# Another written order of steps, and PSUM as one tile whose banks the list schedule hands out

## The chip, the cores and the metric

The kernel runs on one core of a Trainium2 chip. A core has a tensor engine (PE), a vector engine (DVE), a scalar engine (ACT), GpSimd (POOL) and a sync engine (SP), each with its own queue of instructions that it works off in order, and 16 DMA engines. PE writes its products to PSUM, a small memory of eight banks of 128 x 512 fp32 values; DVE and ACT read them from there. Engines wait for each other through semaphores. The metric is the device time of one execution in microseconds; less is better.

## The reference

An attention with exponential features, then a mixture of eight experts whose routing weights are normalized by eight rounds over rows and columns.

```python
def phi(x):                                   # x: 8 x 8 x 576 x 64
    proj = np.einsum('bhsd,df->bhsf', x, w_phi)
    proj = proj - np.max(np.abs(proj), axis=-1, keepdims=True)
    return np.concatenate([np.exp(proj), np.exp(-proj)], axis=-1)
q_p, k_p = (phi(q), phi(k))
kv = np.einsum('bhsf,bhsd->bhfd', k_p, v)
z = np.sum(k_p, axis=2)
num = np.einsum('bhsf,bhfd->bhsd', q_p, kv)
den = np.einsum('bhsf,bhf->bhs', q_p, z)[..., None] + 1e-06
x = (num / den)                               # as 4608 x 512
P = np.exp(x @ w_gate - logits_max)           # 4608 x 8
for _ in range(8):
    P /= P.sum(1, keepdims=True) + 1e-09
    P /= P.sum(0, keepdims=True) + 1e-09
    P *= N / E
for e in range(8):
    out += P[:, e:e + 1] * (np.maximum(x @ w1[e], 0.0) @ w2[e])
```

## The kernel before

The Python program does not issue instructions as it goes. Each piece of work is recorded as an `Op` of a `Plan`, with its engine, a guessed duration, what it reads and writes, and the buffers that it takes. `Plan.schedule` then walks through a list schedule: again and again it takes, of all operations whose inputs are there, the one that can start first by the guessed durations, and among equals the one recorded first. The instructions are issued in that order, so it fixes the order of every engine's queue. The guessed durations serve that order alone; on the chip an instruction starts when its semaphores say so.

Buffers come from rings: a `Ring` has a name, a shape and a number of slots, and a `Buf` is one use of a slot. A `Buf` gets its slot when its first operation is scheduled and gives it back after its last. In before the PSUM is a ring "P1" of eight slots, one bank each, with a tile of its own for each use; a second ring "P2" of double width has none. `Plan.start` asks whether slots are free and from when; `schedule` takes the slot with the earliest time of becoming free. An operation that touches a bank which another engine touched last starts after that one.

The attention works on 32 pairs of heads, four in each of the eight batches, in these steps, one letter each:

- "a" (`pair_a`, `scores`): the products of the keys with w_phi (line 407, `P<-wphi,qkT`), the maxima of their absolute values on DVE (line 399), four exponentials on ACT (line 403), and v scaled by the exponentials of the maxima on POOL (lines 532 and 537). It also issues the loads for the next batch.
- "q" (`queries`): the same for the queries, once with rows and once with features on the partitions.
- "r" (`rest_a`): keys and queries of the last 64 rows of a batch.
- "b" (`pair_b`): the product of k's features with v (line 407, `P<-v,k`), its copy out of PSUM, kv (line 587), and the numerators and denominators of the queries (lines 606 to 631). Line 587 is the "kv copy", one to a pair, 32 in all.
- "c" (`pair_c`): the transposes into xT (lines 645 and 648).
- "g" (`rest_c`, `gate`): the transposes of the last rows and the routing logits of a batch.

Two more letters are the first expert on batches that are done: "u" (`up0`) is eight matmuls of 512 columns into two banks with the ReLU on ACT (line 699), "d" (`down0`) eight matmuls into one bank, copied out by ACT (line 734) or DVE (line 741). The string `order` (line 814) says in which order these steps are recorded, and so which of two ready operations goes first. After it the routing runs on DVE, while PE works off what is left of the first expert. Then come the other seven experts, by products of 256 columns with sums and differences (line 1019, lines 927 to 1181), in a fixed order of its own. The weights of the experts, v, and intermediate results travel by DMA from the queues of POOL and SP.

Of the kernel before, what the change touches and what calls it, by code (L numbers as in the profile page):

```python
# [9 lines left out]
FP32 = mybir.dt.float32  # L10
# [7 lines left out]
class Buf:  # L18


    def __init__(self, ring):
        self.ring, self.t, self.slot, self.left, self.end = ring, None, None, 0, 0.0
        self.last = None

    def __call__(self):
        if self.t is None:
            self.t = self.ring.make(self.slot)
        return self.t


class Ring:


    def __init__(self, pool, shape, dtype, tag, bufs, psum=False):
        self.psum = psum
        self.free = [(0.0, i) for i in range(bufs)]
        self.make = lambda i: pool().tile(shape, dtype, name=tag, tag=f"{tag}_{i}")

    def new(self):
        return Buf(self)  # L40


class Op:
    __slots__ = ("eng", "dur", "lat", "nbytes", "fn", "left", "ready", "users", "idx", "end",
                 "bufs", "deps", "shared")

    def after(self, user):

# [5 lines left out]
class Plan:  # L54
# [43 lines left out]
    def start(self, o, free):  # L98

        t = max(free, o.ready, self.port if o.shared else 0.0)  # L100
        need = {}
        for b in o.bufs:
            if b.slot is None:
                n = need[b.ring] = need.get(b.ring, 0) + 1
                if len(b.ring.free) < n:
                    return None
                t = max(t, sorted(b.ring.free)[n - 1][0])
            elif b.last is not None and b.last.eng != o.eng:
                t = max(t, b.last.end)
        return t  # L110

    def schedule(self):
        ready = {}
        free = {}
        dma_free = 0.0
        for o in self.ops:
            if o.left == 0:
                ready.setdefault(o.eng, []).append(o)
        done = []
        while len(done) < len(self.ops):  # L120
            best = None
            for eng, rq in ready.items():
                f = free.get(eng, 0.0)
                if best is not None and f > best[0]:
                    continue
                for o in rq:
                    t = self.start(o, f)
                    if t is not None and (best is None or (t, o.idx) < best[:2]):
                        best = (t, o.idx, o)
            assert best is not None, "no operation can start"  # L130
            at, _, o = best
            ready[o.eng].remove(o)
            for b in o.bufs:
                if b.slot is None:
                    s = min(b.ring.free)
                    b.ring.free.remove(s)
                    b.slot = s[1]
            free[o.eng] = at + o.dur
            if o.shared:
                self.port = at + o.dur  # L140
            if o.nbytes:
                dma_free = max(at + o.dur + 1.0, dma_free) + o.nbytes / 1e3
                o.end = dma_free + 1.0
            else:
                o.end = at + o.dur + o.lat
            for b in o.bufs:
                if b.ring.psum:
                    b.last = o
                b.left -= 1
                b.end = max(b.end, o.end)  # L150
                if b.left == 0:
                    b.ring.free.append((b.end, b.slot))
            done.append(o)
            for u in o.users:
                u.left -= 1
                u.ready = max(u.ready, o.after(u))
                if u.left == 0:
                    ready.setdefault(u.eng, []).append(u)
        return done
# [9 lines left out]
def kernel(  # L169
# [33 lines left out]
    ps = ctx.enter_context(tc.tile_pool(name="ps", bufs=1, space=PSUM))  # L203
# [6 lines left out]
    P = const.tile([128, NT, E], FP32, name="P")  # L210
# [30 lines left out]
    def pool(el, fn, r=(), w=()):  # L241
        plan.op("POOL", el * 1.64e-3 + 0.17, 0.25, fn, r, w, shared=True)
# [5 lines left out]
    R = {}  # L248

    def ring(p, shape, dtype, tag, bufs):  # L250
        R[tag] = Ring((lambda: p) if not isinstance(p, str) else (lambda: late[p]),
                      shape, dtype, tag, bufs, p is ps)
# [31 lines left out]
    ring("s_p", [128, NT], FP32, "rr", 1)  # L284
    ring("s_p", [128, E], FP32, "cs", 1)
    ring("s_p", [128, E], FP32, "c_bc", 1)
    ring(ps, [128, 1024], FP32, "P2", 0)
    ring(ps, [128, 512], FP32, "P1", 8)

    def new(tag):  # L290
        return R[tag].new()

    def bf(buf):

# [111 lines left out]
    def mm(out_, lhsT, rhs, start, stop):  # L406
        nc.tensor.matmul(out_, lhsT=lhsT, rhs=rhs, start=start, stop=stop)  # L407
# [339 lines left out]
    for b in range(2):  # L747
# [58 lines left out]
    def stage_g(b):  # L806
# [5 lines left out]
             "c": lambda j: pair_c(j // 4, j % 4, xbs[j]), "g": stage_g,  # L812
             "u": lambda i: up0(i // 4, i % 4), "d": lambda i: down0(i // 4, i % 4)}
    order = (
        "aqraqabbcqabqacbqrbcaqbacuqaqbacqruabgqccucbudbduaqabdqadgrcbucqucabqcauqdua"
        "bgcbqaducdcqubcrbaudqauqdacbcdqduardqbbgcubuaqcaubgcdqacdqabubruqadbqadcbqbu"
        "cagcquaubqrdbadqaudbcqcaucbdcccqbgcg"
    )
    for i, n in enumerate(order):
        STEPS[n](order[:i].count(n))  # L820
# [22 lines left out]
    o = plan.op("X", 0.0, 0.0, swap, w=["late"])  # L843
# [270 lines left out]
    def down7(e, g, hT, B7):  # L1114
# [38 lines left out]
        def read(bank, i, j):  # L1153

            if e == 0:
                return start(bank, i, j)
            for n in range(2):
                ts = 2 * i + n
                dve(330, lambda n=n, ts=ts: nc.vector.scalar_tensor_tensor(  # L1159
                    out=acc[g][:, ts, 256 * j:256 * j + 256],  # L1160
                    in0=bank()[:, 256 * n:256 * n + 256], scalar=P[:, 4 * g + ts, e:e + 1],
                    in1=acc[g][:, ts, 256 * j:256 * j + 256], op0=ALU.mult, op1=ALU.add),
                    [bank, "P"], [("acc", g, ts, j)])
# [113 lines left out]
```

## Time and profile before

| | us |
|---|---|
| median of three runs (lowest, highest) | 1043.96 (1043.56, 1044.01) |
| span of the profiled execution | 1043.5 |
| PE busy | 1020.4 (98%) |
| DVE busy | 823.9 (79%) |
| ACT busy | 711.1 (68%) |
| POOL busy | 461.5 (44%) |
| idle time of PE | 23.1 |

The span is the time from the first to the last instruction of the profiled execution, which is another one than the three that were timed. A row of the timeline gives the start of a group of equal instructions, their time, engine, line, operation, what is written and read, the shape and the number. A row of the groups gives busy time, the mean of one, and the idle time of the engine ahead of them with what ended it. The granted clock of PE was 1.00 throughout.

### The profile page before, as it was taken

To read this page: it belongs to the slowest core of one execution; us is meant where nothing else is said; L and a number is where in the kernel's file an instruction comes from. 1 tells how busy PE (TensorE), PEld (TensorE's weight loads), DVE (VectorE), ACT (ScalarE), POOL (GpSimd) and SP (SyncE) were. 2 spreads that over 40 slices of the span, in tenths; PEclk is the share of its full clock that TensorE was granted. 3 is DMA by queue.
4 is the path that set the end of the run, shared out by engine and by line. 5 is a ranking of instruction groups with operands and counts; after the bars stand their busy time and mean duration, and the time that the engine had idled before them with its cause. 6 is when DMAs were issued, how large, how long until landed. Compare 5 with 4: busy or idle time off the path is not lost.

```text
span 1043.5 us, 24529 instructions
## 1 busy us (share of the span) xinstructions
PE 1020.4 (98%) x9512; PEld 842.1 (81%) x9512; DVE 823.9 (79%) x1626; ACT 711.1 (68%) x1570; POOL 461.5 (44%) x532
## 2 busy tenths in 40 slices
PE   6899999999999999999999999999999999999998
PEld 4566666654788888888888888888888888888886
DVE  6999899998777787778877787778777877787775
ACT  7999999944976666666666666565666666666663
POOL 3876757500233344344444444444444443333442
PEclk9999999999999999999999999999999999999999
DMA  9997987734411152113311441134111611114333
GB/s 250 150 196 132 150 127 136 122 122 120 93 41 41 52 105 60 51 42 82 81 41 42 87 87 51 42 69 95 41 42 50 125 51 42 41 43 131 122 122 122
DMA packets 105237, 93.94 MB, mean 90 GB/s; under 512 B 45344, under 2 KB 80288, under 8 KB 105120
## 3 DMA queue, kind: packets, MB, share of 16 engines
q1 hardware_dynamic: 71840, 68.45, 23.6%
q0 software_dynamic: 33120, 23.86, 16.4%
q8 instruction: 74, 1.21, 0.5%
q14 instruction: 43, 0.35, 0.1%
q10 hardware_dynamic: 160, 0.07, 0.0%
HBM read 94.98 MB, written 14.16 MB: 105 GB/s over the span
## 4 chain that ended last, share of the span: by engine, by line
PE 89%; ACT 5%; DVE 3%; DMA 1%; issue 1%; SPq 0%; POOL 0%; DVEq 0%; ACTq 0%
PE P L1019 70%; PE P L407 16%; ACT acc L1181 2%; DVE m L399 1%; PE P L606 1%; ACT k L403 1%; DMA acc<-in_q_dram 1%; DMA wgate_f<-in_moe_w_gate_dram 1%; ACT V L1171 1%; ACT U L1047 1%; PE P L645 1%; DVE xb L626 0%; ACT q L403 0%; DVE P L618 0%; PE P L484 0%
## 5 line engine op out<-in xcount | busy, mean ns | idle before, releaser
L1174 POOL TENSOR_TENSOR acc<-acc,V 128x512 f32<-128x512 f32 x248 | 316.4, 1283 | 440.4 <-ACT V L1171 437.2
L1051 DVE CUSTOM_DVE_ANT_0 hT<-P,U 128x512 bf16<-128x512 f32 x378 | 255.0, 687 | 107.9 <-ACT U L1047 59.7
L1047 ACT COPY U<-P 128x512 f32<-128x512 f32 x378 | 217.8, 590 | 137.4 <-PE P L1019 130.8
L1171 ACT ACTIVATE V<-P,P 128x256 f32<-128x256 f32 x496 | 206.3, 477 | 123.4 <-PE P L1019 121.6
L1159 DVE SCALAR_TENSOR_TENSOR acc<-P,P,acc 128x256 f32<-128x256 f32 x372 | 160.1, 478 | 73.4 <-PE P L1019 71.7
L1019 PEld LDWEIGHTS <-w 128*128 128x128 bf16 x2016 | 197.3, 98 | 23.7 <-issue 0.6
L1019 PEld LDWEIGHTS <-S 128*128 128x128 bf16 x1984 | 194.1, 98 | 23.2 <-issue 0.6
L1019 PEld LDWEIGHTS <-T 128*128 128x128 bf16 x1512 | 147.9, 98 | 19.1 <-issue 2.0
L1019 PEld LDWEIGHTS <-hT 128*128 128x128 bf16 x1488 | 145.4, 98 | 18.3 <-DVE hT L1051 1.1
L1019 PE MATMUL P<-X,w 128*128 128x256 bf16 x1008 | 154.7, 273 | 0.4 <-ACT U L1047 0.4
L1019 PE MATMUL P<-xT,w 128*128 128x256 bf16 x1008 | 152.0, 273 | 0.0
L1019 PE MATMUL P<-X,T 128*128 128x256 bf16 x1008 | 148.6, 273 | 1.3 <-ACT U L1047 1.2
L1019 PE MATMUL P<-w,hT 128*128 128x256 bf16 x992 | 142.6, 273 | 0.6 <-DVE hT L1051 0.6
L1019 PE MATMUL P<-T,S 128*128 128x256 bf16 x1056 | 136.3, 273 | 0.4 <-ACT V L1171 0.4
L1019 PE MATMUL P<-w,S 128*128 128x256 bf16 x928 | 126.6, 273 | 0.0
L532 POOL TENSOR_TENSOR v<-v_m,em 128x512 bf16<-128x512 f32 x64 | 66.8, 1043 | 70.6 <-ACT em L403 57.5
L399 DVE TENSOR_REDUCE m<-P 128x4 f32<-128x512 f32 x128 | 82.7, 681 | 1.7 <-PE P L407 1.2
L1056 ACT ACTIVATE hT<-P 128x512 bf16<-128x512 f32 x126 | 74.6, 607 | 12.9 <-PE P L1019 12.4
L407 PE MATMUL P<-w,hT 128*128 128x512 bf16 x320 | 80.2, 379 | 0.3
L927 DVE TENSOR_TENSOR S<-hT 128x1024 bf16<-128x1024 bf16 x124 | 80.1, 683 | 0.0
L407 PE MATMUL P<-xT,w 128*128 128x512 bf16 x288 | 76.2, 379 | 1.2 <-ACT kr L403 0.5
L1019 PE MATMUL P<-xT,T 128*128 128x256 bf16 x504 | 76.3, 273 | 0.0
(94 smaller groups left out, 1091.7 us busy)
## 6 DMA issues: line engine op xcount, KB each, us to landing
X<-xd SPq DMA_DIRECT2D x126, 256.0 KB, 2.6
w<-in_moe_w_dram POOLq DMA_DIRECT2D x14, 1024.0 KB, 10.4
v_m<-in_v_dram SPq DMA_DIRECT2D x15, 512.0 KB, 5.1
out_dram<-acc SPq DMA_DIRECT2D x14, 512.0 KB, 3.2
xd<-S SPq DMA_DIRECT2D x18, 256.0 KB, 2.0
qk<-in_k_dram POOLq DMA_DIRECT2D x12, 256.0 KB, 5.5
qk<-in_q_dram POOLq DMA_DIRECT2D x12, 256.0 KB, 6.4
w<-in_moe_w_dram POOLq DMA_DIRECT2D x8, 256.0 KB, 7.5
```

Source lines behind the costliest of these rows:

```text
L399: dve(el, lambda: nc.vector.tensor_reduce(out=dst(), in_=src(), axis=AX.X, op=ALU.max, apply_absolute_value=True), r, w)
L407: nc.tensor.matmul(out_, lhsT=lhsT, rhs=rhs, start=start, stop=stop)
L532: pool(512, lambda y=y, em=em: nc.gpsimd.tensor_tensor(out=s["v"][y]()[:, :, 0:D], in0=t["v"]()[:, h0:h0 + 2].rearrange("p a (b c) -> p (a ...
L927: lambda: f.tensor_tensor(out=out_(), in0=x(), in1=y(), op=op), r, w, **kw)
L1019: pe(256, lambda i=i, k=k, z=z: nc.tensor.matmul(bank()[:, 256 * i:256 * i + 256], lhsT=lhs(k, i), rhs=rhs(k), start=first and z, stop=k = ...
L1047: act(512, lambda: nc.scalar.copy(out=u[fp][n]().rearrange("p a b -> p (a b)"), in_=x[fp]()), [x[fp]], [u[fp][n]])
L1051: dve(500, lambda: nc.vector._custom_dve(ADD_SAT, out=out_(fp, i, j), in0=bank[fp]().rearrange("p (a b) -> p a b", a=2), in1=u[fp][n](), s ...
L1056: act(512, lambda: nc.scalar.activation(out=out_(fp, i, j), in_=x[fp]().rearrange("p (a b) -> p a b", a=2), func=ACT.Relu, bias=0.0, scale ...
L1159: dve(330, lambda n=n, ts=ts: nc.vector.scalar_tensor_tensor(out=acc[g][:, ts, 256 * j:256 * j + 256], in0=bank()[:, 256 * n:256 * n + 256 ...
L1171: act(390, lambda n=n: nc.scalar.activation(out=u()[:, n, :], in_=bank()[:, 256 * n:256 * n + 256], func=ACT.Copy, bias=0.0, scale=P[:, 4 ...
L1174: pool(670, lambda: nc.gpsimd.tensor_tensor(out=acc[g][:, 2 * i:2 * i + 2, 256 * j:256 * j + 256], in0=acc[g][:, 2 * i:2 * i + 2, 256 * j: ...
L1181: act(512, lambda ts=ts: nc.scalar.activation(out=acc[g][:, ts, :], in_=acc[g][:, ts, :], func=ACT.Copy, bias=0.0, scale=P[:, 4 * g + ts, ...
```

## The change

Two things. The string `order` is another one, of the same 188 letters: 32 each of a, q, b and c, eight each of r and g, 24 of u and 20 of d. And the PSUM is one tile of 128 x 4096 values; a use is a slice of it, and a new class `Banks` hands out the slices. Of the banks that are free at the moment when the operation could start, it takes the one with the fewest free neighbours, and among these the lowest number; if none is free, the one that becomes free first. A use could be several banks wide; in this kernel all uses are one bank wide.

```diff
+class Banks:
+    psum = True
+    count = 8
+    def __init__(self, make):
+        self.free = {i: 0.0 for i in range(self.count)}
+        self.make = make
+    def find(self, bufs, t):
+        free, slots = dict(self.free), []
+        for b in bufs:
+            best = None
+            for s in range(self.count - b.width + 1):
+                span = range(s, s + b.width)
+                if any(i not in free for i in span):
+                    continue
+                at = max(t, max(free[i] for i in span))
+                near = sum(i in free and free[i] <= at for i in (s - 1, s + b.width))
+                if best is None or (at, near, s) < best:
+                    best = (at, near, s)
+            if best is None:
+                return None
+            t, _, s = best
+            slots.append(s)
+            for i in range(s, s + b.width):
+                del free[i]
+        return t, slots
...
@@ Plan.start
-                n = need[b.ring] = need.get(b.ring, 0) + 1
-                if len(b.ring.free) < n:
-                    return None
-                t = max(t, sorted(b.ring.free)[n - 1][0])
+                need.setdefault(b.ring, []).append(b)
...
+        for ring, bufs in need.items():
+            got = ring.find(bufs, t)
+            if got is None:
+                return None
+            t = got[0]
+            o.slots += zip(bufs, got[1])
@@ Plan.schedule
-            for b in o.bufs:
-                if b.slot is None:
-                    s = min(b.ring.free)
-                    b.ring.free.remove(s)
-                    b.slot = s[1]
+            self.start(o, free.get(o.eng, 0.0))
+            for b, s in o.slots:
+                b.ring.take(b, s)
@@ the kernel
-    ring(ps, [128, 1024], FP32, "P2", 0)
-    ring(ps, [128, 512], FP32, "P1", 8)
+    psum = ps.tile([128, 8 * 512], FP32, name="P", tag="P")
+    banks = Banks(lambda s, w: psum[:, 512 * s:512 * (s + w)])
     def new(tag):
-        return R[tag].new()
+        return banks.new(int(tag[1])) if tag in ("P1", "P2") else R[tag].new()
...
     order = (
-        "aqraqabbcqabqacbqrbcaqbacuqaqbacqruabgqccucbudbduaqabdqadgrcbucqucabqcauqdua"
-        "bgcbqaducdcqubcrbaudqauqdacbcdqduardqbbgcubuaqcaubgcdqacdqabubruqadbqadcbqbu"
-        "cagcquaubqrdbadqaudbcqcaucbdcccqbgcg"
+        "raqaqabbccqaqbbaqrbaccuqrbgaqaquabcucbqccaruqbcabqdaqbacbugdqdaqubdccuubauacuqqd"
+        "drcbagubqbdaqrduabccauqccubqdcbcuadgqgrbuadqbacaudqbqaddcbaurqcuqbcaadubqauabdqd"
+        "gbuccdaqdqbdcbqcuuacbgcqcbcg"
     )
```

The other buffers' rings keep their rule: the slot that has been free longest. The gate and the routing, the experts' order, the shapes and every instruction's operands but for the bank are as before.

More of the change, by code (lines that the diff above doesn't have):

```diff
@@ L18, with __init__ @@
 class Buf:
-    def __init__(self, ring):
+    def __init__(self, ring, width=1):
         self.ring, self.t, self.slot, self.left, self.end = ring, None, None, 0, 0.0
-        self.last = None
+        self.last, self.width = None, width
     def __call__(self):
         if self.t is None:
-            self.t = self.ring.make(self.slot)
+            self.t = self.ring.make(self.slot, self.width)
         return self.t
 class Ring:
-    def __init__(self, pool, shape, dtype, tag, bufs, psum=False):
-        self.psum = psum
+    psum = False
@@ L36, in __init__ @@
+    def __init__(self, pool, shape, dtype, tag, bufs):
         self.free = [(0.0, i) for i in range(bufs)]
-        self.make = lambda i: pool().tile(shape, dtype, name=tag, tag=f"{tag}_{i}")
+        self.make = lambda i, w: pool().tile(shape, dtype, name=tag, tag=f"{tag}_{i}")
     def new(self):
         return Buf(self)
+    def find(self, bufs, t):
+        if len(self.free) < len(bufs):
+            return None
+        got = sorted(self.free)[:len(bufs)]
+        return max(t, got[-1][0]), [s for _, s in got]
@@ new lines, in take, with give, new, find @@
+    def take(self, b, s):
+        self.free = [f for f in self.free if f[1] != s]
+        b.slot = s
+    def give(self, b):
+        self.free.append((b.end, b.slot))
+class Banks:
[4 more added lines that the diff above has]
+        self.make = make
+    def new(self, width=1):
+        return Buf(self, width)
+    def find(self, bufs, t):
+        free, slots = dict(self.free), []
[16 more added lines that the diff above has]
+        return t, slots
+    def take(self, b, s):
+        b.slot = s
+        for i in range(s, s + b.width):
+            del self.free[i]
+    def give(self, b):
+        for i in range(b.slot, b.slot + b.width):
+            self.free[i] = b.end
@@ L43 @@
 class Op:
     __slots__ = ("eng", "dur", "lat", "nbytes", "fn", "left", "ready", "users", "idx", "end",
-                 "bufs", "deps", "shared")
+                 "bufs", "deps", "shared", "slots")
     def after(self, user):
@@ L103, in start @@
             if b.slot is None:
-                n = need[b.ring] = need.get(b.ring, 0) + 1
-                if len(b.ring.free) < n:
-                    return None
-                t = max(t, sorted(b.ring.free)[n - 1][0])
+                need.setdefault(b.ring, []).append(b)
             elif b.last is not None and b.last.eng != o.eng:
                 t = max(t, b.last.end)
+        o.slots = []
+        for ring, bufs in need.items():
+            got = ring.find(bufs, t)
+            if got is None:
+                return None
+            t = got[0]
+            o.slots += zip(bufs, got[1])
         return t
@@ L151, in schedule @@
                 if b.left == 0:
-                    b.ring.free.append((b.end, b.slot))
+                    b.ring.give(b)
             done.append(o)
@@ L251, in ring @@
         R[tag] = Ring((lambda: p) if not isinstance(p, str) else (lambda: late[p]),
-                      shape, dtype, tag, bufs, p is ps)
+                      shape, dtype, tag, bufs)
     ring(wp, [128, 4, FF], BF16, "w1", 2)
```

## The prediction

> **What bounds the kernel now.** I first read the page's totals and, cut by stage, the busy time of each engine in stretches of the span. The cuts are the first and the last kv copy of the attention (line 587), the end of the expert-0 filling, the start of the even stretch, and the start of the last product.
>
> ```profile
> span 1043.5 us, 24529 instructions
> 0.00:20.90 20.90, 12.28 (x88) 9.11 (x88) 13.39 (x26) 13.83 (x37) 8.24 (x22) 1.00 0.90 239
> 20.90:214.00 193.10, 185.84 (x2104) 120.86 (x2104) 176.75 (x441) 180.37 (x466) 126.77 (x251) 1.00 0.89 145
> 214.00:257.60 43.60, 43.60 (x265) 21.88 (x264) 37.86 (x104) 17.09 (x30) 0.82 (x1) 1.00 0.38 129
> 257.60:298.20 40.60, 37.87 (x307) 29.70 (x306) 30.04 (x52) 40.52 (x78) 9.67 (x8) 1.00 0.44 89
> 298.20:1032.10 733.90, 733.87 (x6721) 657.58 (x6721) 561.82 (x1003) 459.27 (x960) 315.96 (x252) 1.00 0.26 68
> 1032.10:1043.50 11.40, 6.92 (x33) 2.94 (x30) 4.00 (x7) 0.00 (x0) 0.00 (x0) 1.00 0.48 185
> ```
>
> The columns are length, then PE, weight loads, DVE, ACT and POOL busy, the granted clock, DMA share and GB/s. From 298.2 to 1032.1 us PE is busy 733.87 of 733.90 us: nothing an order does there can gain, only a new PE wait can lose. From 257.6 to 298.2 ACT is the bound (40.52 of 40.60). From 214 to 257.6 PE is (43.60 of 43.60). Between the first and the last kv copy no engine is alone: PE, DVE and ACT all show over 90%. The time of this stretch is what an order can change, so I went into it.
>
> ```profile
> L587 DVE CAST kv<-P x32: 398/419/429, 20.9 to 214.0; 128x260 bf16<-128x260 f32 x32
> 99.47 0.62 ACT L403 ACTIVATE k<-P 128x512 bf16<-128x512 f32 x1
> 104.59 2.08 ACT L403 ACTIVATE k<-P 128x512 bf16<-128x512 f32 x4
> 104.65 0.68 DVE L399 TENSOR_REDUCE m<-P 128x4 f32<-128x512 f32 x1
> 105.58 1.28 DVE L399 TENSOR_REDUCE m<-P 128x4 f32<-128x512 f32 x2
> 103.02 0.38 PE L407 MATMUL P<-w,hT 128*128 128x512 bf16 x1
> 108.93 1.89 PE L407 MATMUL P<-w,hT 128*128 128x512 bf16 x8
> 105.25 0.42 DVE L587 CAST kv<-P 128x260 bf16<-128x260 f32 x1
> ```
>
> An instruction's own duration overlaps the next one's start, so "busy" flatters. What one more instruction costs its queue is the difference: an exponential (2.08 - 0.62)/3 = 0.49 us (0.48 as the median over all that follow each other), a maximum 1.28 - 0.68 = 0.60, a 512-column matmul (1.89 - 0.38)/7 = 0.216. I took such an interval for each shape and multiplied by the instructions that stand between the first and the last kv copy: PE 172.4, ACT 172.2, DVE 170.1 us, in 193.1 us that it takes (20.9 to 214.0, first row above). The three are evenly loaded, and 20.7 us go to engines waiting for one another. That is the most that an order could ever gain; how much it could lose has no such limit.
>
> **The change, part by part.** Against the built program: every engine has the same instructions in both kernels, with the same shapes. After the last attention matmul 198 matmuls of expert 0 are left in both, and the DVE and ACT queues are the same through the routing and into expert 1. So nothing moves between the stages of the first table; the stages behind the attention shift as a block, and only their banks differ. SP's and POOL's DMA issues keep their order but for a few neighbours. Two terms remain.
>
> *The written order.* It holds the same steps, and the matmuls of expert 0 (line 407 with w) lie elsewhere. Up to the last kv copy both issue 364 of them. I cut both queues at every second kv copy, and give for each piece the number of expert-0 matmuls and the work of PE/ACT/DVE in us, intervals times counts; the time it took is known for before alone.
>
> | kv copies | before: matmuls, PE/ACT/DVE | took | after: matmuls, PE/ACT/DVE |
> |---|---|---|---|
> | 6-8 | 24, 11.7/12.3/12.2 | 13.8 | 19, 11.0/12.4/11.8 |
> | 12-14 | 24, 11.0/10.3/9.7 | 11.4 | 35, 13.5/11.5/11.5 |
> | 14-16 | 46, 16.2/15.0/13.8 | 16.7 | 26, 11.3/11.3/10.9 |
> | 16-18 | 45, 16.1/13.1/11.1 | 16.0 | 25, 11.3/9.9/9.4 |
> | 18-20 | 21, 10.5/10.4/10.3 | 11.2 | 35, 14.6/16.0/14.3 |
> | 22-24 | 21, 10.2/10.8/10.5 | 10.8 | 34, 13.4/10.9/12.3 |
> | 24-26 | 23, 10.6/10.8/10.7 | 11.4 | 29, 11.2/10.3/9.6 |
>
> The largest of the three is a floor for a piece, and the pieces of before took little more than it. Summed over all pieces the floors go from 184.3 to 185.5 us with cuts at even copies, and from 185.6 to 189.4 at odd ones: +1.2 and +3.8, mean +2.5. Why a cut of two pairs: the attention's buffers (k, q, v, kv, qkT) are twofold, so an engine can run about two pairs ahead. With a cut at each pair it is 189.2 to 193.7, +4.5; at every fourth, where the queues are free to slide, 183.3 to 183.9, +0.55. The excess over the floors in before, 193.1 - 185.0 = 8.1 us, I leave as it is. I take **+2.5 us**, and 0.55 and 4.5 as its ends; a gain isn't excluded, since a floor isn't a schedule (below). DVE also gets 35 more pure waits (128 to 163) in the attention. The idle time ahead of its commonest instruction there, the maxima, bounds what such waits cost:
>
> ```profile
> L399 DVE TENSOR_REDUCE m<-P 128x4 f32<-128x512 f32 x128 | 82.7, 681 | 1.7 <-PE P L407 1.2 <-ACT k L403 0.4
> L532 POOL TENSOR_TENSOR v<-v_m,em 128x512 bf16<-128x512 f32 x64 | 66.8, 1043 | 70.6 <-ACT em L403 57.5
> qk<-in_q_dram POOLq DMA_DIRECT2D x12, 256.0 KB, 6.4
> qkT<-qk SPq DMA_TRANSPOSE x12, 5.3
> ```
>
> 1.7/128 = 13 ns each, so 35 of them are under 0.5 us, inside the range. POOL's 54 loads stay in order, but the order moves some past up to 13 of POOL's own instructions, 13 x 1.04 = 13.5 us at the longest. A q/k half is issued four pairs ahead of its use, 4 x 193.1/31 = 24.9 us, and needs 6.4 + 5.3 = 11.7 to land and be turned, so 13.2 us are free: only the most-moved load uses its cover up. Uncovered, the maxima, the exponentials and PE's scores of that pair would wait, for what is missing of it; I take nothing.
>
> *The banks.* The old ring hands out the bank that has been free longest; the new one takes, of all banks free at that planned moment, the one with the fewest free neighbours and the lowest number. One tile instead of many adds no wait of its own: PE's waits on DVE and ACT fall from 799 and 791 to 744 and 769, each for an access that its data or its bank needs. What shrinks is the distance: matmuls of other banks between the last one that fed a bank and the first that overwrites it. The worst place of the expert stage, with the times of before:
>
> ```profile
> 603.62 0.49 PE L1019 MATMUL P<-w,S 128*128 128x256 bf16 x3
> 603.95 0.60 PE L1019 MATMUL P<-xT,w 128*128 128x256 bf16 x4
> 605.41 1.25 DVE L1159 SCALAR_TENSOR_TENSOR acc<-P,P,acc 128x256 f32<-128x256 f32 x3
> 521.53 0.38 PE L1019 MATMUL P<-xT,w 128*128 128x256 bf16 x2
> 522.05 0.69 DVE L1051 CUSTOM_DVE_ANT_0 hT<-P,U 128x512 bf16<-128x512 f32 x1 [1.28 <-PE P L1019]
> ```
>
> The last w,S product ends at 603.62 + 0.49 = 604.11, its reader at 605.41 + 1.25 = 606.66: 2.55 us. The new program has 20 matmuls there, 20 x 0.109 = 2.18: short by 0.37. The usual place is the second pair of rows: fed until 521.91, read until 522.74, 0.83 us against 12 x 0.109 = 1.31, so 0.48 to spare. I did this for each reuse. In the attention the distances hardly differ, since nearly all banks are taken (medians 2.4 and 2.2 us). In the filling up to 257.6 the smallest margin falls from 2.0 to 0.47 us: no wait. In 257.6 to 298.2 the shortfalls sum to 0.4 us, under ACT's bound, where PE has 40.60 - 37.87 = 2.7 us of idle time. In the even stretch the smallest of 529 margins falls from 1.02 to -0.37, with one below zero: 0.4 us. A signal takes 0.14 (521.91 to 522.05); counting all margins under 0.5 as lost to that gives 4.2 us as the far end, and 0 is the near one, since a full PE can't gain. I take **+0.4**, as all but one row has room.
>
> The Trainium skill, "Perfetto Trace Analysis", section "Matmuls", says that independent groups should rotate through the banks so that one group's evacuation overlaps the next group's matmuls. The old ring is that rotation and the new rule turns back to the same low banks; by the page this should lose time, by the rows just shown the distances left are still enough in all but one place.
>
> **The sum.** 1043.5 + 2.5 + 0.4 = 1046.4 us of span. The three runs' median, 1043.96, is 0.5 above this execution's span, so 1046.9 us.
>
> **The rivals.** *Faster: the bunch goes.* Between copies 14 and 18 (105.25 to 138.00) before issues 91 matmuls of expert 0; PE has 32.3 us of work in 32.7 us there while ACT has 28.1, and the chain of waits is PE's.
>
> ```profile
> 127.02 3.00 PE P L407 x29
> 134.31 3.67 PE P L407 x32
> 138.00 0.43 DVE kv L587
> ```
>
> The new order has 51 there and no four pairs with more than 66. If their new neighbours absorb them in the 20.7 us that are lost to waiting, the stretch falls to ACT's 28.1: -4.2 us, 1043.96 - 4.2 + 0.4 = 1040.2. For it: the bunch is the one place where one engine alone set the pace, and maxima that stand last in a bank, behind both its exponentials (2 x 0.48 us), fall from 50 of 80 to 41, so POOL's scaled values, which wait 57.5 us for ACT in the row above, can come sooner. Against it: the floors rise elsewhere, at 18-20 to 16.0. *No change:* the queues slide freely over four pairs, +0.55 + 0.4, 1044.9. For it: the totals are equal. Against it: twofold buffers. *Much slower: banks.* The distances were worked out with the readers' times of before; if the readers come later and all margins under 0.5 us are lost in the even stretch, +4.2, with the pair-by-pair floors +4.5: 1043.96 + 8.7 = 1052.7. It decides as soon as a reader is late by 0.5 us; against it, DVE has 562 and ACT 459 of 734 us of work there and can catch up. *The change doesn't do what it says*, in that one tile makes products wait for each other: the counted waits exclude it.
>
> **How the numbers follow.** Forecast (slower by 1 to 5 us) 0.40, faster 0.32, no change 0.21, banks 0.07. Faster or slower means by over 0.2%, 2.1 us, about what a measurement of this kernel can tell from no change. The forecast's lower end (a rise under 2.1) goes to "same", as do faint gains. That gives faster 0.31, same 0.25, slower 0.44. The likeliest case alone spans 1044.9 to 1049; since both signs hold weight, the range reaches from just under the faster case, 1039.5, to the banks' end, 1052.7.
>
> **What would show it.** Right: the last kv copy comes 1 to 5 us after 214.0, the pieces 18-20 and 22-24 take 16 and 13 us, piece 14-18 falls from 32.7 to some 23, and the block behind moves by the same amount, PE still over 733 of 734 us in its even stretch. Wrong: the last kv copy at 210 or earlier (the bunch was the cost), or the same time there and an even stretch that is longer by over 1 us with waits of PE on DVE (lines 1051, 1159) or ACT (1171) (the banks were).

## The result: faster by 3.1 us, and the profile after

| | before | after |
|---|---|---|
| median, us (20 runs each, same chip) | 1044.89 | 1041.80 |
| lowest and highest | 1043.56, 1046.76 | 1040.22, 1046.56 |
| ratio, 95% interval | | 0.9971 [0.9963, 0.9978] |
| span of the profiled execution | 1043.5 | 1040.0 |

The forecast was 1046.9 us, slower. The time lies inside the range, near its lower end, and on the other side of no change: the kernel became faster.

The first line of after's page, and then the busy times in the stretches that answer to those of the prediction. The cuts are the first and the last kv copy (now line 647), and behind it the old cuts moved by 3.5 us; columns as in the prediction.

```profile
span 1040.0 us, 24497 instructions
0.00:21.16 21.16, 11.79 (x87) 8.85 (x88) 13.35 (x25) 14.04 (x37) 8.44 (x23) 1.00 0.89 242
21.16:210.22 189.06, 180.61 (x2070) 120.81 (x2103) 176.84 (x440) 179.61 (x466) 126.39 (x250) 1.00 0.94 147
210.22:254.10 43.88, 43.58 (x261) 22.07 (x265) 37.78 (x102) 17.09 (x30) 0.82 (x1) 1.00 0.38 129
254.10:294.70 40.60, 38.05 (x307) 29.69 (x306) 30.05 (x52) 40.45 (x78) 9.58 (x8) 1.00 0.43 88
294.70:1028.60 733.90, 733.76 (x6721) 657.63 (x6721) 559.15 (x1003) 460.36 (x961) 315.93 (x252) 1.00 0.26 68
1028.60:1040.00 11.40, 6.85 (x31) 2.94 (x30) 4.46 (x8) 0.00 (x0) 1.04 (x1) 0.93 0.48 184
```

Only one stretch changed its length. From first to last kv copy it took 189.06 us instead of 193.10, and everything behind came that much sooner: from the last kv copy to the end it is 829.5 us in before and 829.7 in after, and the 733.9 us of the even stretch hold the same 6721 matmuls, with PE busy 733.76. DVE and ACT did the same work in the shorter stretch (176.84 and 179.61 us, against 176.75 and 180.37). What shrank is their idle time: 16.4 to 12.2 us on DVE, 12.7 to 9.5 on ACT, each the length less the busy time. PE's busy time there can't be compared: 33 of its matmul records are missing (2070 matmuls beside 2103 weight loads). The run e1 below has the same order and all its records (9512 matmuls beside 9512 weight loads): there PE is busy 182.41 of 189.63 us, so its idle time is 7.2 us as in before (7.3), and it is its busy time that is 3.4 us less, for the same matmuls. PE's busy time in this view is no measure of its work.

Where inside the stretch? Three parts, cut at kv copies 0, 14, 18 and 31; the first fence is before, the second after.

```profile
20.90:105.25 84.35, 78.60 (x916) 51.99 (x917) 78.86 (x198) 79.61 (x205) 59.34 (x116) 1.00 1.01 166
105.25:138.00 32.75, 32.75 (x309) 19.85 (x308) 26.21 (x63) 29.60 (x75) 21.91 (x42) 1.00 1.04 160
138.00:214.00 76.00, 74.49 (x885) 49.03 (x882) 71.68 (x183) 71.16 (x187) 45.52 (x94) 1.00 0.69 115
```

```profile
21.16:108.22 87.06, 79.75 (x903) 53.00 (x917) 80.36 (x199) 81.64 (x212) 60.41 (x117) 1.00 1.07 164
108.22:130.97 22.75, 22.54 (x270) 15.37 (x272) 21.38 (x54) 21.98 (x58) 17.59 (x35) 1.00 1.15 164
130.97:210.22 79.25, 78.31 (x903) 52.44 (x917) 75.10 (x188) 75.99 (x199) 48.39 (x99) 1.00 0.73 125
```

The bunch is gone: copies 14 to 18 fell from 32.75 to 22.75 us, by 10.0. The expert-0 matmuls that left went to both sides, where 2.7 and 3.25 us were added. That looks like the rival "the bunch goes", in size and place; the experiments ask whether it was the cause. The views of waits in the stretch show how the change appears to DVE and ACT (waiting instruction <- what it waited for: us in all, times, longest). Before:

```profile
DVE kv L587 <- PE P L407: 4.8, 5, 1.8
DVE P L618 <- PE P L606: 2.6, 4, 0.9
ACT q L403 <- PE P L606: 4.1, 8, 0.8
```

After:

```profile
DVE kv L647 <- PE P L467: 1.1, 2, 0.9
DVE P L678 <- PE P L666: 0.6, 2, 0.3
ACT q L463 <- PE P L666: 0.7, 3, 0.3
```

In these rows, all of step "b", DVE and ACT stood waiting for PE for 11.5 us in before and 2.4 in after. In the first two DVE waits for products that it reads (v with k, and the numerators). In the third ACT waits to overwrite the features q, of which there are two buffers and which the numerators still have to read. Other rows rose, as ACT's waits for line 407 ahead of k did (1.5 to 2.9 us). Over all rows DVE's waits fell from 14.3 to 9.4 us and ACT's from 10.6 to 8.4, and those for PE among them from 12.2 to 6.3 and from 9.4 to 7.2. This says where the time was saved and not why: with the same work in a shorter stretch, DVE and ACT must be idle for less.

### The profile page after: what moved, and what is told of

It reads as the page before. It is cut to its first block, busy times and chain, and to the rows that moved or that the text cites. A ratio compares the mean times of both kernels' runs of the same rounds, so it can differ in the third digit from the quotient of the medians.

```text
span 1040.0 us, 24497 instructions
## 1 busy us (share of the span) xinstructions
PE 1014.6 (98%) x9473; PEld 842.0 (81%) x9512; DVE 821.6 (79%) x1626; ACT 711.6 (68%) x1570; POOL 462.2 (44%) x532
## 4 chain that ended last, share of the span: by engine, by line
PE 89%; ACT 3%; DVE 3%; DMA 3%; issue 1%; SPq 0%; DVEq 0%; ACTq 0%
PE P L1079 71%; PE P L467 16%; ACT acc L1241 2%; DMA acc<-in_q_dram 1%; DMA qkT<-qk 1%; PE P L666 1%; DVE m L459 1%; ACT V L1231 1%; PE P L705 1%; ACT U L1107 0%; SPq L389 0%; DVE xb L686 0%; ACT hT L1116 0%; DVE P L678 0%; PE P L671 0%
## 5 line engine op out<-in xcount | busy, mean ns | idle before, releaser
L1231 ACT ACTIVATE V<-P 128x256 f32<-128x256 f32 x496 | 205.8, 476 | 134.7 <-PE P L1079 123.5
L1079 PEld LDWEIGHTS <-S 128*128 128x128 bf16 x1984 | 194.1, 98 | 23.1 <-issue 0.6
L1219 DVE SCALAR_TENSOR_TENSOR acc<-P,acc 128x256 f32<-128x256 f32 x372 | 159.3, 478 | 54.4 <-PE P L1079 51.9
L467 PE MATMUL P<-w,hT 128*128 128x512 bf16 x301 | 77.6, 379 | 1.2 <-DVE m L459 0.2
L467 PE MATMUL P<-xT,w 128*128 128x512 bf16 x270 | 73.3, 379 | 1.1 <-DVE m L459 0.2
## 6 DMA issues: line engine op xcount, KB each, us to landing
w<-in_moe_w_dram POOLq DMA_DIRECT2D x14, 1024.0 KB, 10.1
```

What stands on the lines that cost most here:

```text
L1079: pe(256, lambda i=i, k=k, z=z: nc.tensor.matmul(bank()[:, 256 * i:256 * i + 256], lhsT=lhs(k, i), rhs=rhs(k), start=first and z, stop=k = ...
L1219: dve(330, lambda n=n, ts=ts: nc.vector.scalar_tensor_tensor(out=acc[g][:, ts, 256 * j:256 * j + 256], in0=bank()[:, 256 * n:256 * n + 256 ...
L1231: act(390, lambda n=n: nc.scalar.activation(out=u()[:, n, :], in_=bank()[:, 256 * n:256 * n + 256], func=ACT.Copy, bias=0.0, scale=P[:, 4 ...
```

## The experiments

All ratios are to before, from runs on the same chip. "Floor" and "excess" are the prediction's: for each piece of two kv copies the largest of PE's, ACT's and DVE's work, summed (cuts at even copies), and what the stretch took beyond it. The floors given here are counted in the order in which each program issues its instructions, with the prediction's intervals. For before this gives 184.5 us, where the prediction has 184.3; for the new order it gives 184.1, where the prediction has 185.5 (more on this in the section on the prediction). "Letters" are those of `order`; OLD and NEW stand for the two strings of the diff.

**The order alone, and the banks alone.**

```diff
@@ e1: before's program, PSUM still a ring of eight tiles
-    order = OLD
+    order = NEW
@@ e2: after's program, PSUM one tile
-    order = NEW
+    order = OLD
```

> Before, with the new written order alone; PSUM stays the ring of eight one-bank tiles. Every queue then has the same instructions in the same order as in after, so only the banks differ from after. If the order makes the gain (theory O): ratio 0.997, last kv copy near 210.2 us as in after (before 214.0), the block behind moved by -3.4 us. If the banks make it (theory K): ratio 1.000, last kv copy near 214.

> After, with the old written order; PSUM is one tile with the new choice of banks. Every queue has the same instructions in the same order as in before, so only the banks differ from before. Theory O: ratio 1.000 within 0.001, last kv copy near 214. Theory K: ratio 0.997. The prediction's own bank term would give +0.4 us behind the attention, ratio 1.0004.

e1: 1041.56 us, 0.9963 [0.9951, 0.9976]. e2: 1045.25 us, 1.0008 [0.9998, 1.0017]. Each has the queues of the kernel whose order it carries, instruction for instruction; only the banks differ. The kv copies of e1, then of e2 (nanoseconds least, median and most; first and last start in us):

```profile
L587 DVE CAST kv<-P x32: 395/418/430, 20.5 to 210.1; 128x260 bf16<-128x260 f32 x32
```

```profile
L647 DVE CAST kv<-P x32: 397/418/430, 20.3 to 213.1; 128x260 bf16<-128x260 f32 x32
```

The last copy comes at 210.1 with the new order, whatever hands out the banks, and at 213.1 with the old one. So the order makes the whole gain, and the banks cost nothing that these runs can tell from zero (their interval ends at +0.17%). In e2's even stretch, however, there is one wait of PE that before doesn't have:

```profile
604.77 0.70 PE L1079 MATMUL P<-xT,w 128*128 128x256 bf16 x5 [0.44 <-DVE hT L1111]
```

It lies where the prediction saw the worst place, and has the size of its 0.4 us, though PE waits there for hT (line 1051 in before) and not for the accumulation that the prediction timed. But e2 isn't the kernel after: with the new order the view of waits lists none there.

**The new places of expert 0 without the new attention, and the reverse.** e3 has the attention's letters of before and the u and d of after, each behind the same number of attention letters as there (but for the first u, three letters later); e4 is the reverse (but for one u and one d, two letters and one later).

```diff
@@ e3
+        "aqraqabbcqabqacbqrbcaqbacuqaqbaucqruabgqcccubbaqabdqagrcbucdqdcaubdqcuuaquabug"
+        "cddbqaccuqbcdrbaduqaqacubcquardqbbugdcbaqcuadbgcqaudcqabddbrquabquacbqbducaguc"
+        "qdadbqurbdaqdabdcqcauucbcccqbgcg"
@@ e4
+        "raqaqabbccqaqbbaqrbaccqrbugaqaqabcucbqccaurqudbducabqdaqdbacbugquaqbccbuaduacq"
+        "qrcbduadgbuqbaqrudabccudaqcdcdubqdcbcaguqugrbauqbadcaqdbqaucbuardqcqdbcaaubqaa"
+        "buqugbcdcadqqudbcbqcuacdbgcqcbcg"
```

> Rings; the attention's letters (a q r b c g) in the old order, the first expert's letters (u d) put behind as many attention letters as in the new order. The two pieces of kv copies 14 to 18 then hold 60 matmuls of expert 0 instead of 91. If the place of the expert-0 work makes the gain (theory F): -2 to -4 us, ratio 0.996 to 0.998. If the order of the attention's own steps makes it (theory S): ratio 1.000 or above. By the prediction's floors (two-pair mean 188.9 against 185.0 us in before): +3.9 us, ratio 1.0037.

> Rings; the attention's letters in the new order, the first expert's letters behind as many attention letters as in the old order. Copies 14 to 18 hold 78 matmuls of expert 0. Theory F: within 1 us of before, ratio 0.999 to 1.001. Theory S: -2 to -4 us, ratio 0.996 to 0.998. By the prediction's floors (190.6 against 185.0 us): +5.6 us, ratio 1.0054.

e3: 1051.09 us, 1.0058 [1.0045, 1.007]. e4: 1051.99 us, 1.0072 [1.006, 1.0085]. Neither half brings a gain; each alone costs 6 to 8 us, so neither theory F nor theory S holds. Their floors, 189.8 and 189.9 us, are about 5 us above those of before; their excess, 11.3 and 12.0, is above its 8.6 too.

**Is it the bunch?** e5 keeps the attention's letters of before and moves 23 of the 44 u and d, so that copies 14 to 18 hold 73 expert-0 matmuls instead of 91. e6 takes after's attention letters and moves 26, so that a bunch of 94 stands there. e7 takes after's and moves 15 toward 25 to 30 in each piece: the evenest of all.

```diff
@@ e5
+        "aqraqabbcqabqacbqrbcaqbacuqaqbacqrabgqcccbbaqauuuddubqaddgrcbcuqucabqcauqduabg"
+        "cbduqacdcqubcrbuaqaqdacbcqarqudddbbudgcubuaqcabgucdqacdqabubruqaddbqaucbqbcagc"
+        "quaubqrdbaqdaubcqcaducbdcccqbgcg"
@@ e6
+        "raqaqabbccqaqbbaqrbaccuqrbgaqaquabcucbqccaruqbcabqdaqbacbgqaudqbcducbaacqqrcba"
+        "dgbuuuuddudqbaqrduabccauqccudubqcbcadgqgrbuaqbacadqbqacbaudddrqcuuqbcaadubqaab"
+        "qudgbduccdaqdqbcbqdcuacbgcuqcbcg"
@@ e7
+        "raqaqabbccqaqbbaqrbaccuqrbgaqaqabccbuuqccarqbucabqdaqbacbugddqaqubdccuubauacuq"
+        "qddrcbagubqbddaqruabccauqccubqducbdcagqgrbuaqbadcaudqbqadducbarqucqbcaadubqaab"
+        "udqgbcdcaqqbudddcbqcuuacbgcqcbcg"
```

> Rings, the attention's letters in the old order, 23 of the 44 letters of expert 0 moved so that the bunch between kv copies 14 and 18 falls from 91 matmuls to 73 and the pieces around it rise (26, 30, 30, 37, 36, 32, 29, 25, 19, 29, 26 against 27, 26, 24, 46, 45, 21, 30, 21, 23, 33, 17). Theory E (evenly spread expert-0 work is what lets the attention run faster): -2 to -4 us, ratio 0.996 to 0.998. Theory T (each order is a fit of attention steps and expert-0 work to each other, and moving about half of the letters breaks it, in whatever direction): +3 to +7 us, ratio 1.003 to 1.007. By the floors (188.9 against 185.0): +3.9 us.

> Rings, the attention's letters in the new order, 26 letters of expert 0 moved so that copies 14 to 18 hold 94 matmuls (46 and 48) as the old order does, taken from the pieces before and behind. Theory E: +3 to +6 us against after, so ratio 0.999 to 1.003. Theory T: as e5, +6 to +10 us against after, ratio 1.003 to 1.007. By the floors (190.5): +5.5 us against before, 1.0053.

> Rings, the attention's letters in the new order, 15 letters of expert 0 moved so that every piece from copy 6 to copy 30 holds 25 to 30 matmuls (after: 19 to 35). Theory E: no slower than after, 0 to -2 us against it, ratio 0.995 to 0.997. Theory T: slower than after by 2 to 5 us, ratio 0.999 to 1.002. By the floors (188.5 against after's 187.4): +1.1 us against after.

e5: 1049.36 us, 1.0049 [1.0036, 1.0061]. e6: 1054.14 us, 1.0094 [1.008, 1.0108]. e7: 1061.43 us, 1.0159 [1.0138, 1.018]. Thinning the bunch cost 0.5%, 5.1 us, and the evenest order is the slowest of all, so evenness (theory E) isn't the cause. Theory T has e5 right; e6 and e7 lose more than it said. e7 loses most at one place, copies 8 to 10, 16.2 us instead of 12.3 in after. The waits of e7 there:

```profile
POOL v L532 <- ACT em L403: 4.0, 1, 4.0
DVE P L618 <- POOL r L564: 3.1, 1, 3.1
ACT k L403 <- PE P L407: 1.8, 1, 1.8
PE P L606 <- DVE P L618: 1.5, 2, 1.3
DVE kv L587 <- PE P L407: 1.4, 1, 1.4
```

It is a ring of waits: DVE for a small copy on POOL, PE for DVE, ACT and DVE for PE, and POOL for ACT. The timeline shows where DVE's longest wait comes from, first e7 and then after:

```profile
77.83 0.18 POOL L564 COPY r<-r_r 128x2 f32<-128x2 f32 x1
78.05 0.91 DVE L618 TENSOR_TENSOR P<-P,r 128x390 f32<-128x390 f32 x2 [3.08 <-POOL r L564]
```

```profile
71.68 0.18 POOL L624 COPY r<-r_r 128x2 f32<-128x2 f32 x1
73.31 0.61 POOL L525 TENSOR_TENSOR vrd<-v_r,em_r 64x256 bf16<-64x256 f32 x1 [1.46 <-ACT em_r L463]
```

The numerators of pair 8 need the small copy of line 564. In e7 it stands on POOL behind the eight instructions of a step "r" (lines 465 and 469, 74.55 to 77.76 us), which no pair before 12 needs, and DVE waits 3.08 us for it. In after it stands ahead of such a step. The late exponentials, for which POOL waits 4.0 us until 84.09, come only then. The clock took part too (last section).

**A control.** e8 has after's attention letters too, and moves 24 u and d by two to five places each, so that every piece holds nearly the number of expert-0 matmuls that it holds in after.

```diff
@@ e8
+        "raqaqabbccqaqbbaqrbaccqrbugaqaqabucucbqccuarqbcabqaqdbuacbgdqduaqbdccubaaucuuq"
+        "qdrcbadgubqbdaqrabduccaqccuubqdcubcadgqugrbadqbacaudqdbqadcubarqcuqdbcaaubuqda"
+        "abqdgbudccaqqbcdbduqcacbgcuqcbcg"
```

> Control: rings, the attention's letters in the new order, 24 letters of expert 0 moved by 2 to 6 places each while the pieces keep nearly the counts of after (21, 31, 32, 27, 28, 37, 27, 32, 28, 23, 26 against 22, 31, 35, 26, 25, 35, 26, 34, 29, 30, 19). Theory E: as after within 1 us, ratio 0.996 to 0.998. Theory T: +4 to +8 us against after, ratio 1.001 to 1.005.

e8: 1045.84 us, 1.001 [1.0001, 1.0019], some 4 us slower than after, at the near end of what theory T said. Its floors are 185.4 us, after's 184.1. Two orders whose floors are 1.3 us apart, with nearly the same number of matmuls in most pieces, took 194.1 and 189.1 us, 5 us apart.

**Crossing the two orders at the place where they agree.** The first 70 letters of both orders are the same letters in another sequence (kv copies 0 to 12), so the orders can be crossed there exactly. e11 takes letters 71 to 140 of the new one.

```diff
@@ e9
+    order = NEW[:70] + OLD[70:]
@@ e10
+    order = OLD[:70] + NEW[70:]
@@ e11: OLD[140:] with its first "a" turned into "u", to keep the counts
+    order = OLD[:70] + NEW[70:140] + "qud" + OLD[143:]
```

> The old and the new written order hold the same letters in their first 70 places, so they can be crossed there without touching anything else. This kernel is the one before with the new order's first 70 letters (kv copies 0 to 12) and the old order's last 118. Up to copy 12 the two kernels took the same time (73.2 us in before, 73.3 in after, summed by pieces of two pairs), and the whole gain lies behind: 69.2 against 63.2 us from copy 12 to 22, 50.9 against 52.4 from 22 to the last. Theory P (the gain is made by the letters at the place where it shows): the first 70 letters give nothing, about 1044.5 to 1046, ratio 0.999 to 1.001; the floors say +1.7. Theory T (steps and fill are fitted to each other over the whole stretch, any crossing breaks it): 1048 or more, ratio over 1.003. Theory B (the head of the new order leaves the queues in a state that the later pieces live on): the gain is here, 1042 or less.

> The kernel before with the old order's first 70 letters and the new order's last 118. Theory P: the whole gain is in the last 118 letters, last kv copy near 210 us, 1040 to 1042, ratio 0.996 to 0.998; the floors are 184.2 against 185.5 in after, so up to 1.3 us better than after is possible. Theory T: the crossing breaks the fit, 1048 or more. Theory B: no gain, 1044 to 1046.

> The kernel before with the new order's letters 71 to 140 alone (kv copies 12 to 22), the old order's first 70 and last 48, of which one 'a' has become a 'u' to keep the counts. Theory P: pieces 12 to 22 take 63 us instead of 69, the rest as in before, so -6 us, unless the pieces behind take back what they hold more of expert 0: 1038 to 1042, ratio 0.994 to 0.998. The floors say 183.9, the lowest of all orders. Theory T: two crossings, 1048 or more. If it comes out between (1043 to 1046), the new tail is part of the gain.

e9: 1044.77 us, 1.0001 [0.9992, 1.0011]. e10: 1046.31 us, 1.0015 [1.0005, 1.0024]. e11: 1047.02 us, 1.0023 [1.0013, 1.0032]. The new head alone changes nothing, the new rest alone costs 0.15%, and both together gain 0.3%. None of the three theories fits all three runs. P fits e9 alone: the gain isn't where it shows. It isn't in the head either (B), and a crossing isn't as dear as 1048 us (T). The stretch behind copy 12, with the same letters, in e10 and then in after:

```profile
93.08:214.64 121.56, 118.57 (x1332) 76.70 (x1330) 108.86 (x273) 112.49 (x290) 72.19 (x145) 1.00 0.81 128
```

```profile
94.44:210.22 115.78, 114.53 (x1308) 76.45 (x1327) 108.76 (x271) 110.59 (x288) 72.08 (x144) 1.00 0.83 134
```

The same DVE work, floors of 114.5 and 114.3 us, and yet 121.56 us against 115.78. The bunch is gone in e10 as well (copies 14 to 18 hold 52 matmuls and take 23.8 us, against 32.75 in before) and nothing is gained: copies 18 to 31 take 83.3 us, where before takes 76.0 and after 79.25. What differs is the sequence inside the queues. The list schedule goes by the planned times at which engines and buffers come free, and the head leaves other ones, so the same letters give other queues: behind the crossing 172 of DVE's 268 instructions of the attention are followed by another one than in after. In e9, whose rest is before's, it is 20 of 269, and the stretch takes before's time. DVE's waits behind copy 12 show the price, in e10 first:

```profile
DVE P L618 <- PE P L606: 3.8, 5, 1.1
DVE m L399 <- ACT k L403: 2.5, 4, 0.8
DVE m L399 <- PE P L407: 1.6, 4, 0.6
```

```profile
DVE P L678 <- PE P L666: 0.3, 1, 0.3
DVE m L459 <- ACT k L463: 1.2, 3, 0.5
DVE m L459 <- PE P L467: 0.6, 1, 0.6
```

7.9 us against 2.1 in these three. That the difference, 5.8, has the size of the loss is no proof of a cause: DVE does the same work in both, so what the stretch takes longer must appear as idle time of DVE. The rows show at which places it does.

**All orders side by side.** The stretch from first to last kv copy, with the waits that the view of waits lists there for DVE and for ACT:

| kernel | floors | took | excess | DVE's waits | ACT's waits |
|---|---|---|---|---|---|
| after | 184.1 | 189.1 | 5.0 | 9.4 | 8.4 |
| e1, new order, ring | 184.1 | 189.6 | 5.5 | 10.4 | 8.5 |
| e2, old order, one tile | 184.5 | 192.8 | 8.3 | 13.7 | 10.1 |
| before | 184.5 | 193.1 | 8.6 | 14.3 | 10.6 |
| e9, new then old | 186.3 | 193.3 | 7.0 | 14.6 | 11.2 |
| e8, moved a little | 185.4 | 194.1 | 8.7 | 14.9 | 11.5 |
| e11, new in the middle | 182.2 | 194.2 | 12.0 | 17.0 | 13.6 |
| e10, old then new | 182.9 | 194.4 | 11.5 | 15.3 | 12.0 |
| e5, bunch thinned | 188.7 | 198.8 | 10.1 | 17.3 | 15.8 |
| e3, new fill alone | 189.8 | 201.1 | 11.3 | 21.2 | 16.7 |
| e6, bunch in new steps | 187.9 | 201.7 | 13.8 | 22.8 | 20.7 |
| e4, new steps alone | 189.9 | 201.9 | 12.0 | 21.7 | 17.2 |
| e7, evenest | 184.2 | 204.9 | 20.7 | 24.5 | 21.7 |

The floors span 7.7 us, the excess 15.7. The floors don't rank the orders: e7 has lower ones than before and is the slowest. DVE's waits do, nearly, but by arithmetic: DVE is busy for 176 to 179 us of the stretch in every order, and the rest of it is idle time. Small differences in this table mean little: after, e1 and e12 have the same attention queues and took 189.1, 189.6 and 190.6 us. In e11 the mean clock in the stretch was 0.996, some 0.8 us of its time.

**A place that is left.** Not a test of the change: 9 of 36 scalings ahead of expert 1 go from ACT to DVE, since ACT was busy all the time from 259 to 293 us of after while PE had idle time.

```diff
+                if ts == 3:
+                    dve(512, lambda ts=ts: nc.vector.tensor_scalar_mul(
+                        out=acc[g][:, ts, :], in0=acc[g][:, ts, :],
+                        scalar1=P[:, 4 * g + ts, 0:1]), ["P", ("acc", g, ts)] + akey(g),
+                        [("acc", g, ts, j) for j in range(2)])
+                    continue
                 act(512, lambda ts=ts: nc.scalar.activation(
```

> Not a test of the change but of the place that it leaves as the last one where PE waits. The kernel after, with 9 of the 36 scalings of acc by P (the loop over ts ahead of expert 1's down product; ScalarE, 25.1 us for 36 in the stretch 253.75 to 302.0 us of after) moved to VectorE, one in four. In that stretch of after ACT was busy 44.78 of 48.25 us and all of the time from 259 to 293, DVE 34.92, PE 45.58, so PE was idle 2.67 us. If ACT sets that stretch, nine scalings fewer free about 9 x 0.70 = 6.3 us of ACT, more than PE's idle time: the gain is 1 to 2.5 us, the first matmul after the stretch comes that much sooner, and the time is 1039 to 1041, ratio to before 0.994 to 0.9965. Rival: DVE's hT operation, for which PE waits through U, comes later by the scalings queued ahead of it, and the time is 1041 to 1044.

e12: 1042.18 us, 0.9977 [0.9968, 0.9987], no better than after and within the rival's 1041 to 1044. The stretch in after, then in e12:

```profile
253.75:302.00 48.25, 45.58 (x374) 36.32 (x374) 34.92 (x60) 44.78 (x87) 12.55 (x11) 1.00 0.37 76
```

```profile
253.75:302.00 48.25, 45.65 (x376) 36.36 (x377) 38.31 (x69) 40.19 (x78) 12.83 (x10) 1.00 0.40 82
```

ACT lost 4.6 us of work and PE gained 0.07. From the stage's first matmul to the one 428 places on, e12 is 0.25 us shorter than after; its last kv copy came 0.5 us later in that execution, and that hides it. So ACT, though busy all the time, didn't set the length of that stretch: with 4.6 us less of its work PE waits for it as long as in after (1.9 us in both). That the scalings were early work that could wait would explain it, but isn't shown. No run here is clearly faster than after.

## Why the prediction was wrong, step by step

- *Only the stretch between the first and last kv copy changes, the rest shifts as a block:* right in time. Matmul 2900 comes 3.4 us sooner and the last but a few, 9471, 3.5. That "only their banks differ" behind the attention isn't so: from about 512 us on, in the experts, the list schedule gives another sequence too, and half of the places in DVE's queue behind the attention hold another operation than in before. The time doesn't show it.
- *The banks, +0.4 with 0 and 4.2 as ends:* inside its ends. With the order held (e2) they cost 0.0008 [-0.0002, 0.0017] of the time, and one wait of PE of 0.44 us is seen; in after the view of waits lists none of PE between 294 and 1031 us, the place with a margin of -0.37 us included. The rule of the Trainium skill ("Perfetto Trace Analysis", section "Matmuls") that groups should rotate through the banks did not decide here: of the far end of 4.2 us nothing is seen.
- *The pieces and their floors:* the counts of matmuls hold, and 14-18 took 22.75 us (23 forecast) and 22-24 13.4 (13). The floors of the new order don't hold. 18-20 took 15.4 us, less than the 16.0 that were called its floor. By the prediction's intervals, ACT's instructions that start in this piece of after's trace make 14.1 us, and those in 22-24 make 12.0, where the table has 16.0 and 10.9. Counted in issue order, the floors are 184.1 at even cuts and 183.9 at odd ones, where the prediction has 185.5 and 189.4; for before it is 184.5 and 185.8 (184.3 and 185.6). So by the prediction's own rule this term is about -1 us, and not +2.5. How its column for ACT came about isn't known.
- *"The excess over the floors in before, 193.1 - 185.0 = 8.1 us, I leave as it is":* this is the step that failed. By even cuts it fell from 8.6 to 5.0 us, -3.6, beside -0.4 for the floors: -4.0, the whole change of the stretch. Over the orders run here the excess went from 5.0 to 20.7 with floors of 182 to 190, so a forecast from the floors held the smaller term and froze the larger. The prediction had named the 20.7 us of mutual waiting as the most that an order could gain, and then gave it no change.
- *The rival "the bunch goes", 1040.2 us:* its size and place came true (last kv copy at 210.22, -3.8 us), but its cause isn't shown. e10 takes the bunch away and gains nothing, e9 keeps it and loses nothing, e5 thins it and loses 5.1 us. So its going isn't enough; whether it is needed stays open, since no order that keeps it came below 192.8 us. The prediction's own sign, "the last kv copy at 210 or earlier (the bunch was the cost)", tied an outcome to a cause that it couldn't tell from another.
- *The maxima that stand last in a bank, 50 to 41 of 80:* not enough either. e5 has 40, e4 44 and e3 47, and all three lose.
- *"From 257.6 to 298.2 ACT is the bound":* not borne out. e12 took 4.6 us of ACT's work away there, and the stretch became 0.25 us shorter.
- *The median 0.5 us above the span:* in the longer series before's median is 1.4 above it; the difference between the kernels doesn't hang on it.

What is shown: the order alone makes the gain, in the stretch of the attention, where DVE and ACT wait less for PE; and it isn't to be had from any one part of the order that was tried. What stays open: which feature of a sequence keeps the waits short. Counts per piece, floors and the going of the bunch don't suffice to explain it, and the runs offer nothing that would forecast it without a profile.

## What to carry to other kernels

In this kernel three in-order queues were evenly loaded, and the work counts of short pieces didn't rank two orders: what the queues lost to each other differed by more than the floors did. So a forecast for a new order in such a place needs a range of the size of the present waits on both sides, not only of the floors. And a floor for a piece is one only if each queue really stands at its cut when the kv copy comes: a piece with a floor of 16.0 us took 15.4 here. The views of waits (who waits for whom) then show where an order loses, as the small copy on POOL in e7, but that waits grow with the time is arithmetic and not a cause. A tuned sequence can be a fit of all its parts: here half of the good order (e10), or the good order with a third to a half of its filler moved a few places, was worse than either whole. And an engine that is 100% busy need not be the bound: in e12 4.6 us less of its work gained 0.25 us.

## What the hardware showed that was not expected

PE's granted clock made the waits in e7 dearer. Its busy times around copies 8 to 10 (the column before the last two is the granted clock):

```profile
76.00:80.00 4.00, 1.35 (x16) 0.70 (x15) 1.81 (x6) 2.36 (x5) 3.47 (x9) 1.00 0.67 150
80.00:82.00 2.00, 1.73 (x19) 1.35 (x20) 1.84 (x6) 2.00 (x5) 0.09 (x1) 0.80 0.91 122
82.00:84.00 2.00, 1.69 (x5) 0.66 (x5) 2.00 (x7) 1.63 (x5) 0.00 (x0) 0.50 1.05 141
84.00:86.00 2.00, 2.00 (x11) 1.08 (x10) 1.57 (x4) 0.23 (x3) 1.91 (x3) 0.84 0.00 0
```

After 4 us in which PE was busy for 1.35, its clock fell to half. By the last row it was back before 85 us: (0.20 + 0.50 + 0.16) x 2 = 1.7 us of PE's time lost, where it wasn't waiting anyway. The longest single gap in these 4 us was 1.29 us, in the timeline's row:

```profile
78.67 0.28 PE L606 MATMUL P<-kv,q 128*128 128x65 bf16 x4 [1.29 <-DVE P L618]
```

The Trainium skill, "TensorE: Matmul & The Clock Gate", section "HAM oscillation — how this bites in real kernels", asks for no idle gaps of PE over about 3.4 us; here the clock fell after several shorter ones, together 2.65 of 4 us. e11's trace shows half the clock once too, for 3.4 us from 19.7 us on, behind a gap of 2.25 us. Yet e7 also has a gap of 2.14 us, up to 199.03 us, with PE busy for 1.30 of the 3.43 us before that, and there the clock stayed at 1.00: what decides isn't shown. The other three runs of e7 had mean clocks of 0.992 to 0.995 and took 1060.95 to 1063.66 us, the profiled one 0.998 and 1057.1, so part of e7's 17 us is clock and differs from run to run. In after and before no 5 us between 10 and 240 us show a clock under 0.995.

A scaling of 128x512 fp32 values by one number a row, SBUF to SBUF, took ACT 25.1 / 36 = 0.70 us and DVE 0.46 (4.1 us for nine):

```profile
L1241 ACT ACTIVATE acc<-acc,P 128x512 f32<-128x512 f32 x36 | 25.1, 787 | 0.9 <-DVE P L946 0.9
```

```profile
L1242 DVE TENSOR_SCALAR acc<-acc,P 128x512 f32<-128x512 f32 x9 | 4.1, 478 | 0.0
```
